# A LayerNorm mean taken off where a product leaves PSUM, instead of by extra matmuls and by centring the weights

## The chip, the cores and the metric

The kernel runs on one core of one Trainium2 chip. The metric is the time of one execution in device microseconds (us), the median of several. Engines are called by their names in the profile: PE is TensorE, PEld its weight loads, DVE VectorE, ACT ScalarE, POOL GpSimd, SP the engine whose queue issues nearly all DMAs.

## The reference, cut to what matters

A Nystrom attention with 32 landmarks per head feeds a LayerNorm and a two-layer MLP with a residual. There are 8 batches, 8 heads, 576 rows, head width 64, so d = 512 and 2048 hidden units.

```
A  = softmax(q @ k_lm.T);  Bm = softmax(q_lm @ k_lm.T);  C = softmax(q_lm @ k.T)
Z  = six steps of Z = 2 Z - Z @ Bm @ Z, from a scaled Bm.T
x  = heads of (A @ Z @ C @ v), side by side           # 576 x 512 per batch
mu = mean(x);  xn = (x - mu) / sqrt(var + 1e-6) * g_ln
out = x + max(xn @ w_ch1, 0) @ w_ch2
```

The kernel doesn't form xn. W1 below is w_ch1 with g_ln and a factor of 16 multiplied in, in fp16. With zt = the 32-row matrix Z (C v) of each head (called landmarks' rows below), x = A zt, so xn @ W1 is A times (zt @ W1), less the mean. The mean of a row of x is A times the row sums of zt, divided by 512. So the mean can be removed in any of three ways: W1's columns are centred (each column less its own mean over d); or the row sum of zt times the negative column mean of W1 is added to the product zt @ W1, as a rank-1 term; that term can be added by a matmul into the same accumulation, or by the operation that copies the product out of PSUM. The division by the deviation follows at the very end, in the copy of the second layer (`finish_block`), since the maximum with zero commutes with a positive factor.

## The kernel before, in words

**Attention, batch by batch or in pairs.** `attention0` treats batch 0 by itself at the start; `attention2` treats the sets (1), (2), (3, 4), (5, 6), (7). Each goes through: landmark scores `psb` and their softmax (`softmax_of`), scores against all keys `psec` (`scores_k`, exponential on ACT, transposed by DVE into `ecT`), the starting matrix (`gram_of`), the product of C and v (`product`, in PSUM tile `pscv`, closed by `product_done` into `cv`), six iterations (`iterate`: some matmuls of 32 x 32 into a PSUM bank, then one DVE operation that gives the next `st`), meanwhile the query scores `ea` (`scores_q`) and their division by their sums (`normalize`: a matmul `psd`, two activations `lns`, and one multiplication, by DVE for batch 1, by POOL for later sets), then `zt` and, from a second PSUM tile `pszc`, its masked form `zcbd`. `rows_of` multiplies `ea` by `zcbd` to get blocks of 128 rows of x; ACT copies each to `xblk`, and DVE takes its statistics (`block_done`: bn_stats and bn_aggr).

**The jobs of the next set.** `Coming` holds the loads (DMA on SP into six staging buffers `stg`), casts (POOL, to `nat`, with sums `asum` and `s` for some tensors) and jobs of a set: `turn` (a DVE transpose, and a small one of `s` with a reduction), `add_up` (two DVE reductions of 0.7 us), `spread` (a matmul on PE that reads the finished `part` tiles, copied by ACT to `lm`). `prepare(after, casts, jobs)` issues so many of each.

**The MLP.** `First(b)` is the first layer: `product_of_heads(f)` for four column groups f of 512 computes zt @ W1 into two PSUM banks (u = 0, 1: two groups of four heads), copied to `m16` in fp16; `chunk(m)`, m = 0 to 15, multiplies it by `ea` into a `psh` tile (pool `ps2`, two buffers, shared with psec, psea, psd, pscv, pszt and pszc), which ACT passes through the maximum with zero into `hT`. Chunk 4 f is the first that needs product f. `second_layer(b)` multiplies `hT` by `w2_16` for one block of 128 rows at a time, 16 matmuls of 512 columns into one PSUM bank, closed by `finish_block` (a DVE scalar_tensor_tensor on `xblk`, then the store on SP). `mlp()` interleaves second layer b with first layer b + 1 and is a stream of units; `fill(n)` draws n units of 512 columns from it. It draws from batch b + 1's first layer only when that batch's rows have begun (`ready`). What is left of the stream runs at the end.

**What sets the order.** All these instructions are kept in the order of the code, on each engine's queue. The list `steps` gives for every `yield` of a set's attention how much of the stream, how many casts and how many jobs follow. A `while` loop ahead of each set issues what jobs are left, with `fill(5)` after each. For batch 0 the order is written out: the loop over m = 0 to 15 issues chunk m, products 1, 2, 3 after chunks 1, 5, 8, W1's column means (`less_mean`: four matmuls with the constant -1/512, copied by ACT to `less(f)`), batch 1's jobs, batch 0's rows, and from m = 10 the second layer of blocks 0 and 1 (`blocks_0_and_1`, PSUM banks 0 and 1, held). Four PSUM banks are handed out in turn by `banks.take`; from batch 1's attention on, bank 3 belongs to the attention, and three are left.

**The mean.** For batches 0 and 1, `row_sums` computes the row sums of zt by four narrow matmuls with the constant `halves`, ACT copies them to `zsum`, and `product_of_heads` adds one matmul of 512 columns per u and f (`bank<-less,zsum` in the profile). During the first eight yields of batch 2's attention `center_w1` adds `less` to W1 in place, an eighth at a time, on DVE (`w<-w,less`); from batch 2 on the product needs no correction. ACT copies the product for u = 0 and for f = 0, DVE the others. The `less` tiles are two of the 14 buffers of `xpool`, in which the `xblk` tiles live; these buffers come free after the centring.

## Time and profile before

| | |
|---|---|
| median of 3 runs | 318.25 us (318.04 to 319.77) |
| the execution profiled | 318.92 us |
| its span, first to last instruction | 317.1 us |
| busy: PE, DVE, ACT, POOL | 280.5, 169.5, 181.7, 126.7 us |
| granted TensorE clock | 0.998 |
| HBM read, written | 36.70, 9.44 MB |

All durations below are from the one execution profiled; what lies outside its span is 1.82 us. In the profile's slices each digit is the busy share in tenths of a fortieth of the span (7.9 us). A row of a group gives engine and operation, the tiles written and read with their shapes, the count, the busy time and the mean duration, then the idle time just before such instructions and what ended it. Most rows name line 69 or 75, since helpers record every operation; the tiles tell them apart. A matmul row's mean (374 ns for 512 columns) is a latency; matmuls overlap, and the time from one to the next is shorter. In the lists in order of time, brackets hold the idle time of the engine before the instruction, and the instruction that ended it.

### The profile page before, as it was taken

What the parts mean: (1) busy time and instruction counts of PE and PEld (TensorE: products, weight loads), DVE (VectorE), ACT (ScalarE), POOL (GpSimd) and SP (SyncE); (2) the same over time, 40 slices, a digit from 0 to 9 for tenths busy, and PEclk for the clock granted to TensorE, in tenths of its full rate; (3) what the DMA queues carried; (4) which work ended last, traced back from release to release, by engine and by line L of the source; (5) the groups of instructions that cost most, each with busy time, mean ns of one, the idle gap of its engine ahead of it and who ended that gap; (6) DMA issues with size and microseconds to landing.
All of it is one profiled execution on the core that took longest, in us unless ns stands there. A gap on an engine that the chain in (4) does not pass through costs nothing. (4 is left out here: it accounts for less than half of the span.)

```text
span 317.1 us, 8209 instructions
## 1 busy us (share of the span) xinstructions
PE 280.5 (88%) x3439; PEld 149.7 (47%) x3439; DVE 169.5 (53%) x378; ACT 181.7 (57%) x315; POOL 126.7 (40%) x155
## 2 busy tenths in 40 slices
PE   8868996887885797887999999989999999999995
PEld 7534652344432344444544544545554456355544
DVE  2654946667898664336994972555442344121112
ACT  3479865178640674876668549576649465444300
POOL 5387748742469974653927423210003000100000
PEclk9999999999999999999999999999999999999999
DMA  7999997459527949600895261111111112213133
GB/s 258 388 389 386 388 235 285 128 131 293 192 55 233 294 118 321 198 2 9 207 277 166 55 169 33 33 35 35 33 37 34 35 34 50 51 33 68 33 87 82
DMA packets 23486, 46.68 MB, mean 147 GB/s; under 512 B 2324, under 2 KB 2584, under 8 KB 23448
## 3 DMA queue, kind: packets, MB, share of 16 engines
q1 hardware_dynamic: 23288, 46.02, 48.4%
q8 instruction: 27, 0.44, 0.6%
q10 hardware_dynamic: 160, 0.13, 0.2%
q14 instruction: 11, 0.09, 0.1%
HBM read 36.70 MB, written 9.44 MB: 146 GB/s over the span
## 5 line engine op out<-in xcount | busy, mean ns | idle before, releaser
L75 PE MATMUL bank<-w,hT 128*128 128x512 f16 (+1 forms) x592 | 151.0, 374 | 0.7 <-DVE m L69 0.4
L69 ACT ACTIVATE hT<-psh 128x576 f16<-128x576 f32 x128 | 81.5, 650 | 46.4 <-PE psh L75 45.4
L75 PE MATMUL psh<-ea,m 128*128 128x288 f16 x512 | 82.8, 286 | 6.4 <-ACT m L69 2.6
L75 PEld LDWEIGHTS <-hT 128*128 128x128 f16 x592 | 54.7, 98 | 48.5 <-issue 9.5
L75 PEld LDWEIGHTS <-m 128*128 128x128 f16 x512 | 49.0, 97 | 39.0 <-ACT m L69 6.3
L69 DVE SCALAR_TENSOR_TENSOR xblk<-bank,rstd,xblk 128x512 f32<-128x512 f32 (+1 forms) x37 | 26.8, 726 | 32.8 <-PE bank L75 32.7
L69 POOL CAST nat<-stg 128x1152 f16<-128x1152 f32 x28 | 33.1, 1194 | 23.8 <-DMA stg<-in_k_dram 9.9
L69 ACT COPY xblk<-bank 128x512 f32<-128x512 f32 (+1 forms) x40 | 23.3, 584 | 24.7 <-PE bank L75 24.6
L69 DVE BATCH_NORM_STATS2 six<-xblk 128x6 f32<-128x512 f32 x36 | 24.7, 686 | 23.0 <-ACT xblk L69 22.9
L69 POOL TENSOR_TENSOR ea<-ea,lns 128x576 f16<-128x576 f16 x12 | 15.4, 1283 | 51.5 <-ACT lns L69 45.1
L69 ACT CAST m<-bank 128x512 f16<-128x512 f32 x40 | 22.6, 586 | 16.5 <-PE bank L75 15.8
L69 DVE CAST m<-bank 128x512 f16<-128x512 f32 x24 | 16.4, 683 | 23.4 <-PE bank L75 21.3
L69 POOL CAST natv<-stg 128x1152 f16<-128x1152 f32 x16 | 18.3, 1162 | 26.5 <-DMA stg<-in_v_dram 23.9
L69 DVE SCALAR_TENSOR_TENSOR st<-st,bank 128x128 f16<-128x128 f16 (+2 forms) x36 | 11.3, 313 | 28.6 <-PE bank L75 28.6
L69 DVE TENSOR_REDUCE part<-xT 128x32 f16<-128x576 f16 x32 | 22.4, 742 | 0.1
L69 DVE STREAM_TRANSPOSE xT<-nat 128x576 uint32<-128x576 uint32 x28 | 21.3, 760 | 0.4 <-POOL nat L69 0.4
L75 PE MATMUL bank<-w,zt 64*32 64x512 f16 x256 | 17.0, 386 | 3.5 <-ACT xblk L69 2.3
L75 PE MATMUL bank<-zcbd,ea 128*128 128x256 f16 (+1 forms) x80 | 15.6, 274 | 3.4 <-ACT m L69 1.7
L69 POOL COPY hT<-hT 128x1024 f16<-128x1024 f16 x4 | 4.1, 1037 | 34.6 <-PE bank L75 26.2
L69 POOL TENSOR_TENSOR asum<-asum 128x256 f32<-128x256 f32 (+1 forms) x24 | 15.4, 643 | 1.9
L75 PEld LDWEIGHTS <-st 32*32 32x32 f16 x448 | 5.7, 89 | 19.2 <-DVE st L69 9.0
L75 PE MATMUL bank<-st 32*32 32x64 f16 (+1 forms) x384 | 9.3, 189 | 6.0 <-DVE st L69 5.9
(113 smaller groups left out, 264.4 us busy)
## 6 DMA issues: line engine op xcount, KB each, us to landing
stg<-in_q_dram SPq DMA_DIRECT2D x16, 576.0 KB, 6.4
stg<-in_k_dram SPq DMA_DIRECT2D x16, 576.0 KB, 7.0
out_dram<-xblk SPq DMA_DIRECT2D x70, 128.0 KB, 2.4
wstg<-in_moe_w_ch_dram SPq DMA_DIRECT2D x16, 512.0 KB, 7.1
stg<-in_v_dram SPq DMA_DIRECT2D x9, 576.0 KB, 5.7
stg<-in_v_dram SPq DMA_DIRECT2D x14, 288.0 KB, 5.5
out_dram<-xblk ACTq DMA_DIRECT2D x2, 64.0 KB, 2.2
out_dram<-xblk SPq DMA_DIRECT2D x2, 64.0 KB, 1.9
```

The costliest lines, as they stand in the source:

```text
L69: return lambda *args, **kw: keep(getattr(self.engine, op)(*args, **kw))
L75: keep(nc.tensor.matmul(o, l, r, start=start, stop=stop, tile_position=(rb, cb), skip_group_check=(skip or cb != 0)))
```

## The change

W1 is no longer centred and there are no row sums by matmul: `row_sums`, `center_w1` and the constant `halves` go. Instead each attention reduces its `pszc` tile over the 64 columns of a head on DVE (`zsum`, one fp32 number per row of the product), ahead of the `zcbd` operations, and `product_of_heads` leaves PSUM for all batches, f and u by one DVE scalar_tensor_tensor: `less(f)` times the row's `zsum`, plus the product. For batch 0's f = 0 this is cut into two halves of 256 columns. Since `less` is now read to the end, its tiles move to the pool of constants, and `xpool` has 12 buffers.

Around it: batch 1's normalisation goes from DVE to POOL. A `turn` job is held back while fewer than i + 3 casts (i being the number of its tensor; at most all of q and k) have been issued, and its step then issues no job. `product` is cut in two parts, j = 0 to 4 and 5 to 8, with a yield between. Batch 1's attention starts at m = 14 of batch 0's loop (scores), and its gram follows after the loop, ahead of the last eight matmuls of `blocks_0_and_1`; before, the scores came after block step 12 and the gram was the first yield of the loop over `steps`. The plan in `steps` has other counts. The diff, its contexts shortened:

```diff
-    halves = const.tile([P, 2], FP16, name="halves")
-    nc.gpsimd.tensor_copy(out=halves[:], in_=mask2[:])
-
     NV = 2
...
     w2_src = moe_w_ch2.rearrange("(m p) d -> p m d", p=P)
-    xpool = ctx.enter_context(tc.tile_pool(name="xpool", bufs=14))
-
-    less_ = [xpool.tile([P, 2, 512], FP16, name="less", tag="xblk") for _ in range(2)]
+    xpool = ctx.enter_context(tc.tile_pool(name="xpool", bufs=12))
+
+    less_ = [const.tile([P, 2, 512], FP16, name=f"less{i}") for i in range(2)]
...
                 MM(pszc[w][ds(cb, 32), :], st[sl, w, LM:], cv[sl, w, :], rb=32 * h, cb=cb)
-        heads[0] = (ea, zt, 0)
+        zsum = asm.tile([P, W], FP32, name="zsum", tag="zsum")
+        for w in range(W):
+            dve.tensor_reduce(out=zsum[:, w:w + 1], in_=pszc[w], axis=AX.X, op=ALU.add)
+        heads[0] = (ea, zt, [(w, zsum[:, w:w + 1]) for w in range(W)])
         yield "zt"
...
             if self.jobs:
-                f, i = self.jobs.pop(0)
+                f, i = self.jobs[0]
+                n = len(self.units)
+                if f == self.turn and 3 * n - len(self.casts) < min(i + 3, 2 * n):
+                    return
+                self.jobs.pop(0)
                 f(i)
...
-        def product(y):
+        def product(y, js=range(NJ)):
             if not pscv_:
...
             pscv = pscv_[0]
-            for j in range(NJ):
+            for j in js:
                 for r in range(2):
...
             for y in range(W // 2):
-                product(y)
+                product(y, range(0, 5))
+                yield False
+                product(y, range(5, NJ))
                 if y + 1 < W // 2:
...
             if W // 2 <= it < W // 2 + W:
-                normalize(ea[it - W // 2], dve if late else pool)
-            if late and it == 4:
-                product(0)
+                normalize(ea[it - W // 2], pool)
+            if late and it in (3, 4):
+                product(0, range(0, 5) if it == 3 else range(5, NJ))
             if late and it == 5:
...
         dve.tensor_copy(out=zt[:].rearrange("p r w l -> p r (w l)"), in_=pszt[:, :, 0:W * LM])
-        for i, b in enumerate(bs):
-            heads[b] = (ea[U * i:U * i + U], zt, U * i)
         pszc = ps2.tile([P, 2, 512], FP32, name="pszc", tag="p2")
...
                    rb=32 * p_, cb=cb)
+        zsum = asm.tile([P, 2, W // 2], FP32, name="zsum", tag="zsum")
+        dve.tensor_reduce(
+            out=zsum[:], in_=pszc[:, :, 0:D * (W // 2)].rearrange("p x (y e) -> p x y e", e=D),
+            axis=AX.X, op=ALU.add)
+        for i, b in enumerate(bs):
+            heads[b] = (ea[U * i:U * i + U], zt,
+                        [(w, zsum[:, w % 2, w // 2:w // 2 + 1]) for w in range(U * i, U * i + U)])
         for w in range(W):
...
-    def center_w1(f, c=0, n=KCH):
-        o = w1_16[:, ds(c, n), ts(f, 512)]
-        dve.tensor_tensor(out=o, in0=o, in1=less(f)[:, None, :].broadcast_to([P, n, 512]),
-                          op=ALU.add)
-
     class First:
...
             self.b, self.hT = b, hTs[b]
-            self.ea, self.zt, self.w0 = heads.pop(b)
-            self.m16, self.sums = {}, None
-
-        def row_sums(self):
-            pss = banks.take([P, U, 4, LM])
-            for u in range(U):
-                for e in range(2):
-                    MM(pss[:, u, ds(2 * (e ^ u), 2), :], halves[:, e:e + 1].broadcast_to([P, P]), self.zt[:, :, self.w0 + u, :])
-            self.sums = asm.tile([P, U, P], FP16, name="zsum", tag="zsum", bufs=1)
-            act(self.sums[:], pss.rearrange("p u k l -> p u (k l)"), AF.Copy, scale=1.0 / P)
+            self.ea, self.zt, self.units = heads.pop(b)
+            self.m16 = {}
...
                 for e in range(2):
-                    for u in range(U):
+                    for u, (w, _) in enumerate(self.units):
                         rows, cb = ds(64 * e, 64), 32 * (2 * (e ^ u) + r)
-                        MM(psm[u][ds(cb, 32), :], self.zt[rows, r, self.w0 + u, :],
-                           w1_16[rows, 2 * u + r, ts(f, 512)], rb=64 * e, cb=cb,
-                           stop=self.sums is None, skip=True)
-            for u in range(U):
-                if self.sums is not None:
-                    MM(psm[u], self.sums[:, u, :], less(f), start=False, skip=True)
-                if u == 0 or f == 0:
-                    scalar.copy(self.m16[f][:, u, :], psm[u])
-                else:
-                    dve.tensor_copy(out=self.m16[f][:, u, :], in_=psm[u])
+                        MM(psm[u][ds(cb, 32), :], self.zt[rows, r, w, :],
+                           w1_16[rows, 2 * u + r, ts(f, 512)], rb=64 * e, cb=cb, skip=True)
+            n = 2 if (self.b, f) == (0, 0) else 1
+            for part in range(n):
+                cols = ts(part, 512 // n)
+                for u, (_, total) in enumerate(self.units):
+                    dve.scalar_tensor_tensor(
+                        out=self.m16[f][:, u, cols], in0=less(f)[:, cols], scalar=total,
+                        in1=psm[u][:, cols], op0=ALU.mult, op1=ALU.add)
...
         l1 = First(b)
-        if b == 1:
-            l1.row_sums()
-            yield 256, 512
         l1.product_of_heads(0)
...
     l1 = First(0)
-    l1.row_sums()
     l1.product_of_heads(0)
...
             next(a0)
-        if 2 <= m < 10 or m == 13:
+        if 2 <= m < 10:
             b1.next_job()
+        if m == 13:
+            b1.next_job()
+        if m == 14:
+            assert not b1.jobs
+            banks.order.remove(3)
+            next(a1)
         if m >= 10:
...
     keep_tail(0)
+    next(a1)
     for m in range(12, MCH):
         blocks_0_and_1(m)
-        if m == 12:
-            assert not b1.jobs
-            banks.order.remove(3)
-            next(a1)
-            deviations(0)
+    deviations(0)
     for u in range(2):
...
-    steps = [[(4, 0, 0)] + 6 * [(3, 0, 0)] + [(4, 1, 0)] + 5 * [(6, 1, 1)]]
-    steps += [[(6, 1, 1)] * 2 + [(6, 1, 1)] * 6 + [(6, 1, 1)] + 5 * [(6, 1, 1)]]
-    steps += [4 * [(5, 1, 0)] + 6 * [(6, 1, 0)] + [(6, 0, 0)] + 10 * [(8, 1, 1)]]
-    steps += [4 * [(9, 1, 1)] + 6 * [(9, 1, 1)] + [(8, 1, 1)] + 10 * [(9, 1, 1)]]
-    steps += [2 * [(12, 0, 0)] + 6 * [(10, 0, 0)] + [(10, 0, 0)] + 5 * [(10, 0, 0)]]
+    steps = [6 * [(3, 0, 0)] + [(4, 0, 0), (4, 1, 0)] + 5 * [(6, 1, 1)]]
+    steps += [[(5, 1, 1)] * 3 + [(6, 1, 1)] * 6 + [(6, 1, 1)] + 5 * [(6, 1, 1)]]
+    steps += [2 * [(4, 1, 0)] + 4 * [(3, 0, 0)] + 6 * [(6, 1, 0)] + [(6, 1, 0)] + 10 * [(8, 1, 1)]]
+    steps += [2 * [(9, 1, 1)] + 4 * [(5, 0, 1)] + 6 * [(9, 1, 1)] + [(8, 1, 1)] + 10 * [(9, 1, 1)]]
+    steps += [3 * [(8, 0, 0)] + 6 * [(10, 0, 0)] + [(10, 0, 0)] + 5 * [(10, 0, 0)]]
     for c, after, plan in zip(sets, sets[1:] + [None], steps):
...
         attention = a1 if c is b1 else attention2(c.bs, c)
-        for i, ((count, casts, jobs), quiet[0]) in enumerate(zip(plan, attention)):
-            if c is sets[1] and i < 8:
-                center_w1(i // 2, 2 * (i % 2), 2)
+        for (count, casts, jobs), quiet[0] in zip(plan, attention):
             fill(count)
...
                 prepare(after, casts, jobs)
```

## The prediction

> **What bounds the kernel now.** I read the page's engine shares and slices first, then its chain.
>
> ```profile
> PE 280.5 (88%) x3439; PEld 149.7 (47%) x3439; DVE 169.5 (53%) x378; ACT 181.7 (57%) x315; POOL 126.7 (40%) x155
> ...
> PE   8868996887885797887999999989999999999995
> DVE  2654946667898664336994972555442344121112
> PE 39%; ACT 4%; issue 1%; DVE 1%; ACTq 0%
> ```
>
> TensorE is nearly full from 170 us on, and the chain runs on it; what it loses (317.1 - 280.5 = 36.6 us) lies mostly before. So a microsecond counts if it leaves TensorE's work or one of its waits. DVE has three stretches at 9 where it may set the pace. Next, the groups with shapes kept apart, for prices (the two columns after the count are busy us and mean ns).
>
> ```profile
> L69 DVE SCALAR_TENSOR_TENSOR xblk<-bank,rstd,xblk 128x512 f32<-128x512 f32 x35 | 25.8, 739 | 30.5 <-PE bank L75 30.4
> L69 ACT CAST m<-bank 128x512 f16<-128x512 f32 x40 | 22.6, 586 | 16.5 <-PE bank L75 15.8 <-ACT lm L69 0.6
> L69 DVE CAST m<-bank 128x512 f16<-128x512 f32 x24 | 16.4, 683 | 23.4 <-PE bank L75 21.3 <-ACT hT L69 2.0
> L69 DVE TENSOR_TENSOR w<-w,less 128x1024 f16<-128x1024 f16 x8 | 6.7, 840 | 0.0
> L75 PE MATMUL bank<-less,zsum 128*128 128x512 f16 x16 | 4.8, 384 | 0.0
> ```
>
> Last, TensorE's and DVE's instructions in order of time (start, duration, and in brackets the idle time before it and its releaser).
>
> ```profile
> 50.10 0.23 PE L75 MATMUL bank<-st 32*32 32x64 f16 x6 [1.30 <-DVE st L69]
> 55.17 0.24 PE L75 MATMUL bank<-st 32*32 32x64 f16 x8 [1.39 <-DVE st L69]
> 56.80 0.24 PE L75 MATMUL bank<-st 32*32 32x64 f16 x8 [0.64 <-DVE st L69]
> 76.90 0.38 PE L75 MATMUL bank<-part,spread 128*128 128x256 f16 x2 [1.21 <-DVE part L69]
> 93.33 0.24 PE L75 MATMUL bank<-st 32*32 32x64 f16 x8 [0.68 <-DVE st L69]
> 96.54 0.22 PE L75 MATMUL bank<-st 32*32 32x32 f16 x8 [1.57 <-DVE st L69]
> 99.45 0.24 PE L75 MATMUL pszt<-st,cv 32*64 32x32 f16 x8 [1.29 <-DVE st L69]
> 53.40 1.52 DVE L69 TENSOR_TENSOR ea<-ea,lns 128x576 f16<-128x576 f16 x1 [1.44 <-ACT lns L69]
> 55.04 1.51 DVE L69 TENSOR_TENSOR ea<-ea,lns 128x576 f16<-128x576 f16 x1
> ```
>
> The iterations of batches 1 and 2 wait for `st` behind other work in DVE's queue: the two normalisations (1.5 us each) in batch 1, the centring of W1 and the next set's jobs in batch 2. At 76.90 DVE is already late for batch 2's `spread`.
>
> **What the Trainium skill says.** VectorE: DVE Perf Modes, "The TRN2 errata", prices a DVE operation out of PSUM at 120 cycles plus one per element: 632 cycles, 0.66 us for 512. The trace is close, 0.683 for the copy and 0.739 for a scalar_tensor_tensor. PSUM — Partial Sum Buffer, "Engine vs sequencer instructions", says VectorE's queue is strict FIFO and matmuls go in program order; the waits above agree. TensorE: Matmul & The Clock Gate, "Back-to-back issue gap", gives N/2.4 + 2.5 ns, 216 ns for 512 columns; the last stretch agrees (64 of 512 and 32 of 256 in 17.32 us: 0.216 per 512). Perfetto Trace Analysis, "Optimizing Scalar/DVE Operations", says work may be moved off a saturated DVE; here it is moved onto it, so the question is where DVE is saturated.
>
> **The change, part by part**, against the profiled execution: 318.92 us, 1.82 of them outside the span of 317.1.
>
> *Rank-1 matmuls and row sums go.* 16 x 0.216 = 3.46 us of TensorE, half in batch 0 and half in batch 1, and about 0.3 for eight narrow matmuls on `halves`: -3.8. ScalarE loses the two `zsum` activations (0.8).
>
> *Centring goes.* Eight operations, 6.7 us of DVE at 81 to 100 us. The TensorE waits there that end with DVE are 0.70 (cv), 0.68, 1.57, 1.29 and 0.77 (zcbd): 5.0. The gate on `turn` jobs also takes out DVE's waits for POOL's `s` (0.96). Bounds -2.5 to -5; some steps still hold a 1.4 us `add_up`, so I take -4.2.
>
> *Batch 1's normalisation goes to POOL.* 1.39 + 0.64 of waits leave: -2.0. POOL's pair (1.28 each in its row) precedes batch 2's casts, which ran at 51 to 62 us and shift by about 5. Their cover: the first `turn` that reads them starts at 62.72 and is gated later still; uncovered they would cost up to 2. Behind them on SP stand loads that need the staging buffers; POOL's waits of 2.2 and 1.1 us for v at 62 to 67 take that up.
>
> *The gram goes up.* Its first half (psb, psec) is issued at m = 14 and its second before the last eight `blocks_0_and_1` matmuls (1.73 us), which cover csum, cinv and st. The 1.30 wait goes, but psec takes both ps2 buffers between chunks 14 and 15 (wait of about 0.65 for hT), and the two finishing operations (1.37) now stand in front of the first iteration's st. Bounds +0.5 to -1.5; taken -0.8. No DMA moves with it; the two stores of blocks 0 and 1 follow as before.
>
> *Copies become scalar_tensor_tensor.* ScalarE loses 40 x 0.586 = 22.6 us. DVE loses 16.4, 6.7 (centring) and 3.0 (normalising) and gains 62 x 0.74 + 4 halves x 0.48 (the row of 256 f32) = 47.8, and about 2.1 for seven `zsum` reductions (0.22 to 0.42 by the 64- to 256-wide rows): 169.5 becomes about 193. The form itself is not in the trace; bounds 0.68 (the copy) and 0.74, and back to back (two in 1.37) a pitch of 0.67. Where this meets a full DVE:
>
> - Batch 0 (24 to 41 us). DVE works through from 27.5 to 41.5 us already. Now 4 halves (1.7) fill its gap before 27.5, and six whole operations (4.0) replace three copies (1.9). Queued in the order of the code, product 3's first one comes after `add_up` 2 and ends near 36.1. Counting the bank takes, product 3 now sits in bank 0, which `blocks_0_and_1` needs; its first matmul was at 35.93. Batch 0's saving (1.73 + 0.15 of row sums) ends in that wait: +1.9.
> - Batch 1 (61 to 77 us). 8 x 0.67 for 3 x 0.62 is +3.5, the reduction +0.25; 1.35 fits into an idle of 2.48 us at 63.5 to 65.9, from which a `turn` (0.75) leaves. DVE is about 3.1 later at `spread`. TensorE issues 43 units of 512 columns before it where it was 35 (+1.7), and is freed of 2.0, so it arrives as before: the wait of 1.21 becomes 4.3. As 1.7 of work comes forward, the net is 1.4, and 3.4 with the 2.0 counted above. Bounds 1 to 5, since DVE can start sooner on what TensorE no longer delays: taken +2.8.
> - Batches 3 and 4's rows (142 to 172 us). DVE is idle 3.5 of 30 us and gets five operations of ScalarE's (3.4) and 0.4 of reduction; 1.35 fits into the wait of 1.96 before 146.01. `spread` at 170.50 has no slack (DVE's last part ends at 170.45). Bounds 0 to 3: taken +1.6.
> - Batch 2's rows: three operations (2.0) and a later job against 2.9 idle: +0.3 (0 to 1.5).
> - Starts of batches 4 to 7: the second matmul of chunk 0 came 1.18 after product 0 (103.70 to 104.88, on ScalarE), now about 1.5: 4 x 0.3 = +1.2.
>
> *The rest.* The split product holds a ps2 buffer through two more fills: +0.3 (0 to 1). A lighter ScalarE shortens waits on hT and xblk: -0.7 (0 to -1.5). xpool at 12 instead of 14: block 31 is taken at 225.9 with blocks 20 to 31 live, so it needs block 19's store, finished by DVE at 225.3 plus 2.4 to land. More units now run ahead of this point, so nothing is taken; if not, up to 2.
>
> Sum: -3.8 - 4.2 - 2.0 - 0.8 + 1.9 + 2.8 + 1.6 + 0.3 + 1.2 + 0.3 - 0.7 = -3.4, say 315.5 for the execution profiled. It stands 0.67 above the median of 318.25, so about 315.0.
>
> **Rivals.**
> - *DVE has the room.* In all it has 124 us free. If batches 1, 3 and 4 cost only 1 together, and batch 0 keeps its 1.9, it is 318.25 - 3.4 - 3.4 - 1.9 = 309.6 at the best, 312 if half. Against: queues are in order, and those stretches are full.
> - *Slower: `spread` waits behind the scalar_tensor_tensors.* At batch 1's and the (5, 6) set's `spread` TensorE stops until DVE's last `turn` is through. With the upper bounds there (5 and 3), and the waits in batch 2's iterations only half gone (-2.5) because `add_up` fills them, the sum is -3.4 + 2.2 + 1.4 + 1.7 = +1.9: 320. It decides once these waits grow by over 3.4 together. For: 76.90 and 170.50 are just where DVE is late or at par.
> - *Nothing gained.* The freed TensorE time turns into waits of the same length: 318.
>
> **How the numbers follow.** The forecast's case (313 to 316.6) has 0.38, the room 0.14, nothing gained 0.16, slower 0.32, with block 31's wait in it. A change under 0.5% (1.6 us) is about what a measurement of this kernel can't tell. Faster 0.52, same 0.16, slower 0.32. The range from 310.0 to 322.0 holds the room's half, and the slower case with another 2 us for block 31. The likeliest case's own range is 313 to 316.6.
>
> **What would show it.** Right: no `less,zsum` or `halves` rows and no `w<-w,less`; m only by DVE, 0.68 to 0.74 each, DVE near 193 us, ScalarE near 158; batch 1's iterations without DVE waits over 0.3; TensorE's wait at batch 2's `spread` grown to 3 or 4 us; a wait for bank 0 near 35 us. Wrong: a scalar_tensor_tensor over 0.8 us; DVE waits under 1 us at each `spread` (then faster than I say); waits for `st` in batch 2's iterations as before, or an xblk wait near 226 (then slower).

## The result, and the profile after

The changed kernel takes 332.51 us (median of 4 runs, 330.86 to 333.58), the kernel before 319.01 on the same chip (318.04 to 319.81): a ratio of 1.042, 95% interval 1.036 to 1.048. It is 4.2% slower; 315.0 was forecast, with 322 as the upper end. Here and below, medians are of all runs, while ratios leave out the runs more than 1.5% above the fastest of their kernel. The execution profiled took 333.58 us, its span 331.9.

The page of the changed kernel: shares, slices with the granted clock, and the chain.

```profile
PE 290.9 (88%) x3415; PEld 151.8 (46%) x3415; DVE 190.8 (58%) x417; ACT 160.8 (48%) x273; POOL 125.1 (38%) x156
...
PE   8988899795896977797988999889988999999995
...
DVE  2656974588489673247898644956743356343112
...
PEclk9956999989899799997999999999999999999999
...
PE 59%; DVE 21%; ACT 11%; DMA 4%; issue 4%; SPq 0%; ACTq 0%; DVEq 0%
```

The busy times of DVE and ACT are close to the forecast ones (193 and 158). The surprise stands in two places. TensorE's *busy* time rose by 10.4 us although 16 matmuls of 512 columns left, while its idle time rose by only 4.4 (36.6 to 41.0). And the row PEclk, all nines before, has holes: the granted clock was 0.958 over the span (0.998 before, where only the last 1.4 us ran at half).

The groups by shape, and the waits of TensorE (total us, times, longest), first of the changed kernel, then of the kernel before:

```profile
L69 DVE SCALAR_TENSOR_TENSOR m<-less,zsum,bank 128x512 f16<-128x512 f16 x62 | 43.2, 738 | 20.8 <-PE bank L75 20.6 <-ACT hT L69 0.2
```

```profile
PE psh L75 <- DVE m L69: 8.3, 16, 1.5
PE bank L75 <- DVE m L69: 5.1, 6, 1.4
PE bank L75 <- DVE part L69: 4.7, 2, 2.8
...
PE bank L75 <- DVE st L69: 1.6, 4, 0.6
```

```profile
PE bank L75 <- DVE st L69: 5.9, 6, 1.6
PE psh L75 <- ACT m L69: 2.6, 10, 0.5
PE bank L75 <- ACT m L69: 2.3, 5, 0.7
...
PE bank L75 <- DVE part L69: 1.2, 1, 1.2
```

The new operation costs the 0.74 us assumed. The rows for `less,zsum`, `halves` and `w<-w,less` are gone. Waits for `st` fell from 5.9 us (and 1.7 at pszt) to 1.6; waits for m are 13.4 us, where before it was 4.9 for ACT's m and about 0.4 for DVE's; waits for `part` 4.7, were 1.2.

The same instants as in the lists in order of time shown for the kernel before, now of the changed kernel, TensorE's queue:

```profile
64.09 0.30 PE L75 MATMUL psh<-ea,m 128*128 128x288 f16 x1 [0.85 <-DVE m L69]
64.75 0.54 PE L75 MATMUL psh<-ea,m 128*128 128x288 f16 x3 [0.36 <-DVE m L69]
...
67.47 1.17 PE L75 MATMUL psh<-ea,m 128*128 128x288 f16 x4
...
69.39 0.65 PE L75 MATMUL psh<-ea,m 128*128 128x288 f16 x4
...
82.03 0.39 PE L75 MATMUL bank<-part,spread 128*128 128x256 f16 x2 [2.85 <-DVE part L69]
...
100.37 0.22 PE L75 MATMUL bank<-st 32*32 32x32 f16 x8 [0.39 <-DVE st L69]
```

Batch 1's iterations wait for `st` only once (0.27 us, at 53.85), batch 2's 0.39 in all, and `spread` waits 2.85. At chunk 0 of batch 1 TensorE stands 0.85 and then 0.36 us for the two scalar_tensor_tensors in a row. Then, with no wait, four matmuls of a chunk take 1.17 us at 67.47 where they take 0.65 at 69.39.

Stretches of 3.4 us of the changed kernel (busy us of PE, PEld, DVE, ACT, POOL with counts, then the granted clock, DMA share, GB/s), in pairs: with a gap, and what followed.

```profile
61.80:65.20 3.40, 1.83 (x15) 0.74 (x15) 2.17 (x4) 0.58 (x1) 3.16 (x5) 1.00 0.64 159
65.20:68.60 3.40, 3.40 (x18) 1.29 (x17) 2.08 (x4) 1.13 (x2) 3.08 (x5) 0.50 1.04 287
78.80:82.20 3.40, 0.55 (x6) 0.33 (x4) 3.11 (x8) 0.87 (x2) 2.84 (x3) 1.00 1.02 392
82.20:85.60 3.40, 3.13 (x54) 1.67 (x56) 0.39 (x2) 2.00 (x4) 3.08 (x6) 0.51 0.95 362
...
150.50:153.90 3.40, 1.43 (x14) 0.64 (x15) 2.18 (x5) 0.65 (x1) 0.00 (x0) 1.00 0.67 174
153.90:157.30 3.40, 3.40 (x12) 1.74 (x12) 3.33 (x6) 1.24 (x2) 1.99 (x2) 0.51 0.00 0
```

In a stretch where TensorE was busy 1.83, 0.55 or 1.43 of 3.4 us nothing is wrong with the clock; the *next* stretch runs at half. There are five such falls before the end, 13.7 us long from 17.4 on and 3.4 us long near 65, 82, 110 and 154: 27.3 us, so 13.7 us of full-speed clock lost.

### The profile page after: what moved, and what is told of

Same layout as the page of the kernel before. It is cut to its first block, busy times and chain, and to the rows that moved or that the text cites. A ratio compares the mean times of both kernels' runs of the same rounds, so it can differ in the third digit from the quotient of the medians.

```text
span 331.9 us, 8161 instructions
## 1 busy us (share of the span) xinstructions
PE 290.9 (88%) x3415; PEld 151.8 (46%) x3415; DVE 190.8 (58%) x417; ACT 160.8 (48%) x273; POOL 125.1 (38%) x156
## 4 chain that ended last, share of the span: by engine, by line
PE 59%; DVE 21%; ACT 11%; DMA 4%; issue 4%; SPq 0%; ACTq 0%; DVEq 0%
PE bank L75 39%; PE psh L75 15%; DVE m L69 6%; ACT hT L69 5%; DVE part L69 4%; DVE six L69 3%; DMA wstg<-in_moe_w_ch_dram 3%; DVE xT L69 3%; ACT xblk L69 2%; DVE xblk L69 2%; PE psd L75 2%; DMA stg<-in_k_dram 1%; PE psec L75 1%; PE pscv L75 1%; ACT lns L69 1%
## 5 line engine op out<-in xcount | busy, mean ns | idle before, releaser
L75 PE MATMUL bank<-w,hT 128*128 128x512 f16 (+1 forms) x592 | 153.9, 378 | 1.6 <-DVE m L69 1.6
L75 PE MATMUL psh<-ea,m 128*128 128x288 f16 x512 | 87.5, 297 | 14.5 <-DVE m L69 8.3
L69 DVE SCALAR_TENSOR_TENSOR m<-less,zsum,bank 128x512 f16<-128x512 f16 (+1 forms) x66 | 44.8, 722 | 22.6 <-PE bank L75 20.6
L69 POOL CAST nat<-stg 128x1152 f16<-128x1152 f32 x28 | 31.9, 1144 | 34.6 <-DMA stg<-in_k_dram 13.7
L69 POOL TENSOR_TENSOR ea<-ea,lns 128x576 f16<-128x576 f16 x14 | 17.9, 1284 | 71.5 <-ACT lns L69 64.7
L75 PE MATMUL bank<-w,zt 64*32 64x512 f16 x256 | 19.3, 406 | 2.9 <-ACT xblk L69 1.8
L69 POOL TENSOR_TENSOR asum<-asum 128x256 f32<-128x256 f32 (+1 forms) x24 | 14.2, 590 | 1.9
L69 POOL TENSOR_TENSOR asum<-nat 128x512 f32<-128x512 f16 x12 | 13.8, 1152 | 1.0
L69 ACT ACTIVATE lns<-psd 128x576 f32<-128x576 f32 x16 | 10.4, 649 | 7.7 <-PE psd L75 7.6
L75 PEld LDWEIGHTS <-zt 64*32 64x32 f16 x256 | 5.1, 89 | 18.8 <-issue 17.4
```

The costliest lines, as they stand in the source:

```text
L69: return lambda *args, **kw: keep(getattr(self.engine, op)(*args, **kw))
L75: keep(nc.tensor.matmul(o, l, r, start=start, stop=stop, tile_position=(rb, cb), skip_group_check=(skip or cb != 0)))
```

## The experiments

Theories. *Queue*: TensorE waits for VectorE, whose queue got longer. Its two forms are *latency* (chunk 0 needs two operations in a row) and *load* (all that stands in VectorE's queue comes later). *Clock*: the waits are short, but each may cost the following 3.4 us half of their clock. *Order*: the moved work is to blame.

How times are compared. In every run the clock lost is (1 - granted clock) x span. Over the 133 runs of the kernel before that were made beside the experiments it is 2.9 us on average, and the time rises by 0.54 us for each microsecond lost (correlation 0.89). Four kernels below with 20 or 22 runs each give 0.56 to 0.61. So a stretch of 3.4 us at half clock (1.7 lost) costs about 1 us. "At full clock" below is the median of a kernel's runs with a granted clock of 1.000 where it has any; else, as an estimate, the mean of its times less 0.57 of the clock each lost ("by the line"). The kernel before: 318.4 at full clock (29 runs). It was run again beside each of the five rounds of experiments, with 318.1 to 318.8 at full clock, so a difference between kernels of different rounds is uncertain by some 0.5 us. The changed one lost 11.8 us on average: 325.6 by the line.

| | median us | ratio, 95% | lost, us | at full clock |
|---|---|---|---|---|
| changed | 332.5 | 1.042 (1.036-1.048) | 11.8 | 325.6 line |
| start filled | 332.4 | 1.043 (1.037-1.050) | 11.3 | 326.3 line |
| waits filled | 329.4 | 1.034 (1.029-1.038) | 0.6 | 329.3 |
| mean alone | 326.9 | 1.024 (1.018-1.031) | 8.1 | 322.1 line |
| order alone | 322.1 | 1.010 (1.007-1.012) | 3.6 | 320.0 |
| fewer fills | 327.4 | 1.021 (1.012-1.030) | 3.9 | 325.1 line |
| f = 0 by ACT | 327.9 | 1.025 (1.019-1.031) | 6.9 | 323.7 line |
| half load | 325.2 | 1.017 (1.010-1.023) | 9.5 | 319.7 line |
| batch 1's order | 325.7 | 1.019 (1.013-1.026) | 5.6 | 322.6 line |
| fitted fills | 325.1 | 1.013 (1.008-1.017) | 1.7 | 324.0 |
| fitted fills, half load | 317.9 | 0.994 (0.991-0.997) | 1.1 | 317.7 |
| before, no mean | 314.5 | 0.978 (0.974-0.982) | 5.3 | 311.7 line |
| order, no mean | 318.4 | 0.993 (0.990-0.996) | 5.5 | 315.5 line |
| POOL normalise | 318.7 | 0.996 (0.993-0.999) | 3.8 | 316.8 |
| order, DVE normalise | 322.8 | 1.011 (1.006-1.016) | 3.7 | 321.1 line |
| mean in 2 batches | 322.6 | 1.007 (1.005-1.010) | 10.1 | 317.0 line |
| POOL normalise, filled | 317.4 | 0.993 (0.991-0.996) | 1.3 | 317.0 |
| mean in 2, filled | 317.0 | 0.992 (0.990-0.995) | 1.6 | 316.1 |

Five of these kernels leave the mean in, in all features or in part of them: f = 0 by ACT, the two with half load and the two with no mean. Their output is not the reference's; they stand here only for their times.

### Is it the clock? Start filled, waits filled

The fill is a few matmuls of a constant, written to a PSUM region that the next real matmul overwrites:

```diff
+    def warm_next(n, cols=256):
+        i = next(i for i in banks.order if i not in banks.held)
+        idle = banks.view(i, [P, 512])
+        for _ in range(n):
+            MM(idle[:, 0:cols], zeros[:, 0:P], zeros[:, 0:cols])
...
                 product(it - 2)
+                if it == 2:
+                    warm_next(8)
                 lns.append(divisors(ea[it - 2]))
```

> The changed kernel, with 8 matmuls of 256 columns of a constant tile (their product is overwritten and used by nothing) set ahead of batch 0's divisors, where TensorE stood 1.25 us before its clock fell to half for 13.5 us. Clock theory (short waits let the granted clock fall, and the half-clock stretches are the loss): the stretch from 17.7 to 31.2 us is gone and with it half of its length, 5 to 7 us: 326 to 328 us, mean clock near 0.98; the four later stretches stay. Queue theory (the loss is the time that TensorE waits for VectorE's m and part): nothing changes, 331 to 334.

Measured: 332.41 us. In the execution profiled the first fall is gone as expected, but its cost is not gone from the time. The slices of this run:

```profile
PEclk9999999898698799997999999999999999999999
```

The four later falls stay, and two of them now last twice as long: 3.4, 6.8, 6.8 and 3.4 us from 64, 81, 105 and 153 us on. The mean loss over the runs is 11.3 us where it was 11.8. So one fall taken away need not shorten the sum of them. Only the profiled executions show where the falls lie; whether the first fall was there in all runs of the changed kernel is not known. The clock theory in the form "each fall costs its half" failed here.

```diff
             psl = banks.take([P, 2, 8, LM])
             for half in range(2):
+                if half == 0:
+                    for _ in range(10):
+                        MM(psl[:, 0, :, :].rearrange("p k c -> p (k c)"), zeros[:, 0:P], zeros[:])
...
             psh = ps2.tile([P, 2, 512], FP32, name="psh", tag="p2")
+            if m == 0:
+                for _ in range(8):
+                    MM(psh[:, 0, 0:256], zeros[:, 0:P], zeros[:])
```

> As the kernel before this one, and with 10 such unused matmuls ahead of each spread and 8 ahead of chunk 0 of every batch, that is inside the waits for part and for m, which are left as long as they are. Clock theory: no stretch under 0.9 is left, mean clock 0.99 or more, 317 to 321 us. Queue theory: the waits are as long as ever and the unused matmuls come on top where a wait was shorter than they are: 332 to 336.

Measured: 329.43, clock 0.995 to 1.000. Both numbers missed: the clock was held, and the time fell by only 3 us. The fill is in the way where the wait was short or absent: the five spreads that had no wait got 1.26 us of unused matmuls each, and each chunk 0 1.04 us, whether it waited or not. So this run shows that the clock can be held, not what it is worth.

### Mean alone, order alone

```diff
-            for u in range(U):
-                if self.sums is not None:
-                    MM(psm[u], self.sums[:, u, :], less(f), start=False, skip=True)
...
+                for u, (_, total) in enumerate(self.units):
+                    dve.scalar_tensor_tensor(
+                        out=self.m16[f][:, u, cols], in0=less(f)[:, cols], scalar=total,
+                        in1=psm[u][:, cols], op0=ALU.mult, op1=ALU.add)
...
-            if c is sets[1] and i < 8:
-                center_w1(i // 2, 2 * (i % 2), 2)
```

The plan of steps, the gram, the normalise and the product stay as in the kernel before.

> The mean's part of the change alone (scalar_tensor_tensor on VectorE, reductions of zsum, less in tiles of its own, 12 block buffers, no rank-1 matmuls, no centring of W1), in the order of work of the kernel before: its plan of steps, batch 1's gram where it was, its normalise on VectorE, no bound on the early jobs, one product of the scores in one piece. Queue theory: VectorE's queue delays part and st as well as m, with batch 1's normalise still in it: slower than the changed kernel's 332.5, 333 to 338. Clock theory: slow only if a wait lets the clock fall; with the waits for m ahead of each chunk 0 still there, 325 to 335 with a mean clock of 0.95 to 0.98. If the order of work is to blame (it was the reordering that made the waits): 316 to 320, clock at 0.99.

> The rest of the change alone: batch 1's gram earlier, its normalise on GpSimd, the product of the scores in two pieces, the early jobs held back, the new plan of steps, on the mean as the kernel before takes it (row sums, rank-1 matmuls, centring of W1, ScalarE and VectorE copies, 14 block buffers). Queue theory and clock theory both: the waits for m return to the kernel before's, clock 0.99 or more, and batch 1's normalise off VectorE gains 1 to 4 us: 314 to 318 us. If the order of work is to blame: over 325.

The second is the converse: the diff above not made, the rest of the change made. Measured: 326.93 and 322.08; at full clock +3.7 and +1.6 against 318.4. Both parts slow the kernel, and the clock loss comes with the mean (8.1 us against 3.6), which fits the clock theory (325 to 335). The order alone fits no theory: it was to gain 1 to 4 us, or to lose over 6. TensorE's waits in its run say why it did not:

```profile
PE bank L75 <- DVE part L69: 4.2, 2, 2.5
PE bank L75 <- DVE st L69: 3.9, 5, 1.6
PE psh L75 <- ACT m L69: 3.9, 11, 1.3
```

`st` fell by 2.0 us from 5.9, `part` rose by 3.0 from 1.2, ACT's m by 1.3. Batch 1's rows begin at 57.5 us where they began at 60.8; batch 2's `spread`, after a wait of 2.48 for 1.21, at 74.9 for 76.9; and batch 2's scores at 78.3 for 78.5. So of the 3.3 us that batch 1 gained, 1.3 are waited for at the `spread`. Nearly all the rest went between there and the scores, where this execution ran at half clock from 74.7 to 78.1.

### Latency or load; fewer fills; batch 1's order

```diff
+            if self.bs[0] == 2 or (self.bs[0] == 3 and y == 1):
+                for _ in range(8):
+                    MM(psl[:, 0, :, :].rearrange("p k c -> p (k c)"), zeros[:, 0:P], zeros[:])
...
+            if m == 0 and self.b in (1, 2, 3):
+                for _ in range(5):
+                    MM(psh[:, 0, 0:256], zeros[:, 0:P], zeros[:])
```

> The changed kernel with unused matmuls only where TensorE waited longer than they take: 8 ahead of batch 0's divisors, 8 ahead of the spread of batch 2 and of the second spread of (3, 4), 5 ahead of chunk 0 of batches 1, 2 and 3. Clock theory: the stretches at half clock near 65, 83, 110 and 154 us go, mean clock 0.985 or more, and the time comes to what the runs so far give for full clock (a line through the changed kernel's times against the clock time it lost, from the first fill run, ends at 326.0): 325.5 to 328. Queue theory alone: 331 to 334, whatever the clock does.

Measured: 327.4, but in two groups: 325.8 and 324.5 with the clock at 0.995 and 0.999, 328.9 and 330.1 at 0.979. The same program differs by over 4 us between the two.

```diff
                 for u, (_, total) in enumerate(self.units):
+                    to = self.m16[f]
+                    if f == 0:
+                        scalar.copy(to[:, u, cols], psm[u][:, cols])
+                        to = self.m16[1]
                     dve.scalar_tensor_tensor(
-                        out=self.m16[f][:, u, cols], in0=less(f)[:, cols], scalar=total,
+                        out=to[:, u, cols], in0=less(f)[:, cols], scalar=total,
```

> The changed kernel with VectorE's load kept and its latency ahead of chunk 0 taken away: of each batch's first 512 hidden features m is written by two ScalarE copies (the mean is left in for these), while VectorE makes the same scalar_tensor_tensors into a tile that is written over. Latency theory (the loss is TensorE standing at chunk 0 until two scalar_tensor_tensors in a row are done, 0.85 + 0.36 us a batch against 0.37 before): 8 x 0.84 = 6.7 us less waiting, and the clock drops that follow chunk 0 (65, 110 and 154 us) go: 322 to 326. Load theory (what counts is VectorE's total work, which delays part and the later m): 330 to 333.

```diff
+                    if f and u == 0:
+                        scalar.copy(self.m16[f][:, u, cols], psm[u][:, cols])
+                        continue
                     dve.scalar_tensor_tensor(
```

> The other way round: chunk 0's two scalar_tensor_tensors stay on VectorE, and of the other three products of each batch the first half goes to a plain ScalarE copy (the mean is left in there): 24 scalar_tensor_tensors of 0.72 us less on VectorE, 17 us. Load theory: the waits for part (4.7 us) and for m ahead of the attention's matmuls (5.1 us) shrink to those of the kernel before, and the clock drop at 83 us goes: 323 to 327. Latency theory: the waits at chunk 0 stay, 330 to 333.

Measured: 327.9 without the latency at chunk 0 and 325.2 with half the load at the other products; by the line 323.7 and 319.7, against 325.6. Load is worth about 6 us, latency about 2 at full clock (and 3 us of clock loss, 11.8 to 6.9 us times 0.57). Both kernels also give ScalarE copies that the changed kernel doesn't have. Neither theory holds alone; load is the larger.

```diff
-                product(y, range(0, 5))
-                yield False
-                product(y, range(5, NJ))
+                product(y)
...
-    steps += [[(5, 1, 1)] * 3 + [(6, 1, 1)] * 6 + [(6, 1, 1)] + 5 * [(6, 1, 1)]]
+    steps += [[(6, 1, 1)] * 2 + [(6, 1, 1)] * 6 + [(6, 1, 1)] + 5 * [(6, 1, 1)]]
...
```

This is against the order alone; the plans of the sets after batch 2 go back likewise.

> The kernel before with only what the change does to the order up to batch 1: gram earlier, normalise on GpSimd, early jobs held back, batch 1's own plan; the plans of batch 2 on and the product of the scores in one piece as before. If the 2.3 us that the whole reordering costs at full clock come from the later plans: 317 to 318.5, at best faster than both kernels. If they come from batch 1's part: 320 to 322. Where batch 2's part is what limits, the 3 us that batch 1 gains come back as a longer wait at its spread (2.5 us in the run of the order alone, 1.2 before).

Measured: 325.7, 322.6 by the line, so the old plans made it worse, not better. That the later plans cost the 1.6 us is refuted. As expected `spread` waited 2.48 us. Batch 2's rows began 3.7 us earlier than in the kernel before (98.3 for 102.0 us), and the lead was gone by the scores of (3, 4) (114.6 for 114.7); later the (5, 6) set took 5.5 us more from scores to rows, with a stretch of 3.4 us at half clock in it.

### What the clock, the load and the mean are worth

```diff
-                for _ in range(8):
+                for _ in range(16 if self.bs[0] == 2 else 12):
...
-                for _ in range(5):
+                for _ in range(9 if self.b == 2 else 6):
```

This is against the fewer fills.

> The changed kernel with unused matmuls sized closer to the waits: 16 ahead of batch 2's spread, 12 ahead of the second spread of (3, 4), 6 ahead of chunk 0 of batches 1 and 3, 9 for batch 2, 8 ahead of batch 0's divisors. Clock theory: clock at 0.99 or more in nearly every run, and the time at 324.5 to 326.5, which is where the lines through the changed kernel and the two fill runs end; so about 6 of the 13.5 us lost were the clock. If the fill itself costs: over 327 with the clock at 1.0.

Measured: 325.08, clock 0.989 to 1.000; 324.0 in the two runs at 1.000. With fills fitted to the waits the changed kernel is 7.4 us faster than without (runs of different rounds), and the forecast of the line holds. TensorE at chunk 0 of batch 1 in this run:

```profile
62.14 0.82 PE L75 MATMUL psh<-zeros 128*128 128x256 f16 x6
63.16 0.30 PE L75 MATMUL psh<-ea,m 128*128 128x288 f16 x1 [0.20 <-DVE m L69]
63.82 0.54 PE L75 MATMUL psh<-ea,m 128*128 128x288 f16 x3 [0.36 <-DVE m L69]
```

The wait of 0.85 is full of unused matmuls, m comes when it came (1.24 us after the last real matmul began, as at 64.09 in the changed kernel), and no fall follows there. Nothing of use was added, so the gain is the clock's: 7.4 us as measured, 5.8 by the line for the 10.1 us of clock regained.

The next one adds the diff of the half load:

> The kernel before this one, and of the second to fourth product of each batch the first half goes to a plain ScalarE copy (the mean is left in there), 17 us less on VectorE. Load theory: the half-load run's own line ends at 319.6 to 320.9 for full clock: 319 to 321.5 here. If that line misled and load is worth little: 323 to 326.

Measured: 317.9, clock 0.989 to 1.000. Against the run before it: 324.0 to 317.7 at full clock, 6.3 us for 24 of the scalar_tensor_tensors. Its slices:

```profile
DVE  2567954686688753169995375655443354321112
PEclk9999999999999999999999999999999999999999
```

```diff
     l1 = First(0)
-    l1.row_sums()
...
-            if c is sets[1] and i < 8:
-                center_w1(i // 2, 2 * (i % 2), 2)
```

> The kernel before without row sums, rank-1 matmuls and centring of W1; its copies, order and buffers as they are. The mean is left in everywhere, so this is the most that any treatment of the mean could gain on this order. The prediction took 3.8 us for the rank-1 part and 4.2 us for the centring: 310 to 311. If the time that they take is covered by batch 2's wait for its sums, as the run of the order alone hints (3 us gained by batch 1, none left at batch 2's spread): 316 to 318.

> The same on the changed order: the order alone (322.1; 320.1 at full clock) without row sums, rank-1 matmuls and centring, the mean left in everywhere. If the removal is worth what the prediction took: 312 to 314. If it is covered: 318 to 320. Against the changed kernel (325.6 at full clock) the difference is the price of 66 scalar_tensor_tensors on VectorE with the order held.

Measured: 314.5 and 318.4; by the line 311.7 and 315.5. On the old order the removal is worth 6.7 us (318.4 to 311.7), on the changed one 4.5 (320.0 to 315.5). The prediction's gain was real, within 1 to 4 us; on the changed order it lies between the two expectations. With the order held, the scalar_tensor_tensors then cost 324.0 - 315.5 = 8.5 us (10.1 by the line), and on the old order 322.1 - 311.7 = 10.4.

### The parts of the order, and a version that is faster

```diff
-                normalize(ea[it - W // 2], dve if late else pool)
+                normalize(ea[it - W // 2], pool)
```

> The kernel before with batch 1's normalise on GpSimd and nothing else. If the normalise is worth what the prediction took (2.0 us less waiting of batch 1's iterations for st): 316 to 317 at full clock, against 318.1 for the kernel before. If the time gained is only waited for at batch 2's spread: 317.5 to 318.5 at full clock. If GpSimd's queue is what costs (its casts of the next batches stand behind the normalise): 319.5 or more.

This is the kernel before with that one line. Measured: 318.7; 316.8 at full clock against 318.2 for the 7 full-clock runs of the kernel before beside it: 1.4 us faster, ratio 0.996 (0.993 to 0.999). Its TensorE in the last iterations of batch 1:

```profile
54.58 0.24 PE L75 MATMUL bank<-st 32*32 32x64 f16 x8
54.75 0.75 PE L75 MATMUL pscv<-natv,ecT 64*32 64x65 f16 x72
55.43 0.82 PE L75 MATMUL bank<-w,hT 128*128 128x512 f16 x3
56.19 0.22 PE L75 MATMUL bank<-st 32*32 32x32 f16 x8
```

The waits of 1.39 and 0.64 us are gone. At batch 2's `spread` the wait is 1.21 us, as long as before, and that set's scores begin at 76.3 for 78.5. So this gain is kept.

> The order alone, with batch 1's normalise left on VectorE. If the normalise on GpSimd is what costs: 317 to 318.5 at full clock, against 320.1 with it on GpSimd. If the earlier gram and the later plans cost: 320 to 322.5.

Its diff is that line turned back in the order alone. Measured: 322.8, 321.1 by the line. The order without the normalise loses 2.7 us against 318.4; the normalise gives back 1.1.

```diff
-                if self.sums is not None:
-                    MM(psm[u], self.sums[:, u, :], less(f), start=False, skip=True)
-                if u == 0 or f == 0:
+                if self.zs is not None:
...
+                        dve.scalar_tensor_tensor(
+                            out=self.m16[f][:, u, cols], in0=less(f)[:, cols], scalar=self.zs[u],
+                            in1=psm[u][:, cols], op0=ALU.mult, op1=ALU.add)
+                elif u == 0 or f == 0:
```

Here `zs`, the row sums, exists for batches 0 and 1 only.

> The kernel before with the row sums and rank-1 matmuls of batches 0 and 1 replaced by 16 scalar_tensor_tensors on VectorE and two reductions; W1 centred and everything else as before. Load theory with the price that the runs give (10 us for 66 scalar_tensor_tensors, so 0.15 us each, 2.4 us for 16) against the rank-1 part's worth (2 to 4 us): 316.5 to 318.5 at full clock. If the waits at chunk 0 of batches 0 and 1 and batch 2's part make more of it: 319.5 or more.

Measured: 322.6 on the median with 10.1 us of clock lost, 317.0 by the line. At full clock that would be 1.2 us less than the kernel before beside it (318.2); as it ran, it is 0.7% slower (the ratio, 1.007). Two stretches of this run and what followed:

```profile
63.20:66.60 3.40, 1.85 (x9) 0.69 (x9) 2.37 (x5) 1.05 (x2) 1.16 (x1) 1.00 0.97 237
66.60:70.00 3.40, 3.27 (x17) 1.53 (x17) 3.25 (x6) 0.98 (x3) 2.32 (x2) 0.50 0.29 100
76.80:80.20 3.40, 0.98 (x9) 0.81 (x9) 3.33 (x9) 0.98 (x3) 2.13 (x2) 1.00 1.03 388
80.20:87.10 6.90, 5.93 (x122) 3.25 (x119) 3.58 (x11) 4.76 (x9) 2.93 (x5) 0.51 0.64 243
```

Whether that 317.0 can be had was the last question.

```diff
+    idle_at = {(1, 0): 9, (2, 4): 5, (2, 5): 11}
...
+            if (bs[0], it) in idle_at:
+                warm_next(idle_at[bs[0], it])
             st = iterate(p1, st, it, W)
```

> The kernel before with batch 1's normalise on GpSimd (318.7 on the median, 316.6 at full clock) and unused matmuls in its longest waits: 8 ahead of batch 0's divisors, 9 ahead of batch 1's first iteration, 9 at batch 2's spread, 5 and 11 at its last two iterations, 9 at zt. Clock theory: clock at 0.995 or more, median 316.5 to 317.3. If the clock is no cause, or the fill costs as much as it saves: 318 to 319.5.

> The same fill, with 6 more unused matmuls ahead of chunk 0 of batches 0 and 1 and 16 at batch 2's spread, in the kernel with the mean by scalar_tensor_tensor in batches 0 and 1 and batch 1's normalise on GpSimd. Clock theory: the line of the run without fill ends at 316.9, less 1.2 for the normalise: 315 to 317 with the clock at 0.99. If the scalar_tensor_tensors in batches 0 and 1 cost by VectorE's queue what the rank-1 part cost on TensorE: 316.5 to 318. If the clock is no cause: 320 to 322.

Measured: 317.4 (clock 0.987 to 1.000) and 317.0 (0.984 to 1.000), ratios 0.993 (0.991 to 0.996) and 0.992 (0.990 to 0.995). Both are 0.7 to 0.8% faster than the kernel before, and cannot be told from each other. The same mean that was 0.7% slower than the kernel before without the fill is 0.8% faster with it and the normalise; the normalise is worth about 1.4 us of this.

## Why the prediction was wrong, by its own steps

**Two steps failed. One is not in the sum: every wait was priced at its own length, and TensorE's clock at nothing. The other is in its terms: the new order of work was taken as a gain and is a cost, and the scalar_tensor_tensors' waits were priced too low.** The clock alone doesn't explain the miss: even at full clock the changed kernel takes 324.0 to 325.6, above the upper end of 322.

The clock first. The page of the kernel before showed 0.998 and a row of nines, and its own waits of 1.2 to 1.6 us had not cost the clock in that execution. But its trace already has eleven stretches of 3.4 us in which TensorE was busy for only 1.84 to 2.44 us. So the sum treats a new wait of 0.85 us as 0.85 us. The run with fitted fills shows 5.8 to 7.4 us that hang on the clock alone (all of the 11.8 lost, times 0.57, is 6.7), of the 13.5 between the two kernels; the kernel before pays about 1.7 of its own (2.9 us lost, times 0.57). The Trainium skill has the mechanism, in TensorE: Matmul & The Clock Gate, "What's actually happening": the array's clock is halved after an idle window of about 3.4 us and comes back after a busy one, and these windows run freely, whenever the kernel starts. The trace agrees on the half, the 3.4 us (3.4, 6.8 and 13.7 us are one, two and four of them) and the shift between runs. The page's "HAM oscillation" puts the danger at idle gaps of over 3.4 us; here the longest was 2.85, and waits of 0.35, 0.85 and 0.36 us in one stretch (61.8 to 65.2) were enough. The measurement decides.

The rest, 324.0 to 325.6 at full clock against 318.4, is 5.6 to 7.2 us slower where the sum has -3.4, so its terms are off by 9 to 10.6 together. One by one:

- *Rank-1 and row sums -3.8, centring -4.2.* Together -8.0; measured -6.7 on the old order, -4.5 on the changed one. Right in kind; that the changed order had already taken a part of it from batches 1 and 2, which could not be taken twice, is likely and not shown.
- *Batch 1's normalisation -2.0.* Right in kind, a third too large or more: -1.4 on the old order, -1.1 on the new, and POOL's later casts delayed nothing: `spread` waited the same 1.21.
- *The gram goes up -0.8, the split product +0.3.* Wrong in sign: the order without the normalise costs 2.7. The prediction priced the gram's own waits and took the new plan of steps at nothing. Of batch 1's gain 1.3 us are waited for at batch 2's `spread` (1.21 to 2.48 us). Which of the moved counts costs the rest was not found; the old plans with the new batch 1 are worse still.
- *Batch 0 +1.9.* Right in place: product 3 sits in bank 0 and its wait is 1.40 us, at 39.7.
- *Batch 1's `spread` +2.8.* The wait grew from 1.21 to 2.85, not to 4.3. Right in place. But it leaves TensorE 0.55 us of work in a stretch of 3.4, and the next one is at half clock.
- *Batches 3 and 4 +1.6, batch 2 +0.3, starts of batches 4 to 7 +1.2.* Too small. The chunks' waits for m are 8.3 us, 5.7 more than for ACT's m before, and not only from batch 4 on; the second `spread` of (3, 4) waits 1.86 where it was 0.47. With 0.7 off for ScalarE, the prediction's costs of the scalar_tensor_tensors are 7.1 us; measured 8.5 to 10.4.
- *xpool at 12.* Right: near 240 us there is a wait of 0.54 for m and none for xblk.

So of the sum's terms the order's was wrong by some 4 us, the gain short by 1 to 4 and the scalar_tensor_tensors' cost by 1 to 3, and the clock added 4 to 6 net of what it takes from the kernel before. Of the rivals, "slower: `spread` waits behind the scalar_tensor_tensors" was right at one of its two places. Its own condition, growth of over 3.4 us together, did not come: batch 2's `spread` waits 1.6 us more and the (5, 6) set's (at 177.1 and 181.6) not at all, while the (3, 4) set's second one, which it did not name, waits 1.4 more. And its 320 left out the clock too. None of the signs named for a slower end came (0.738 us for the operation, 0.39 of `st` waits in batch 2, no xblk wait), and nothing in the list looked at the clock's row. What is argued and not shown: why just these stretches made the clock fall and others did not.

## What to carry to other kernels

A short wait on TensorE has two prices: its length, and the clock of the next microseconds. When a change moves work to another engine, look for stretches of a few microseconds that a new wait would leave half empty, and hold the clock there with unused matmuls that are shorter than the wait; longer ones cost what they take. And compare versions at equal clock too: one kernel here was, by the line, 1.2 us better than the one that it came from at full clock and 0.7% slower as it ran.

## What the runs showed of the hardware that was not expected

- In the changed kernel the clock fell in pieces of 3.4 us (one or four), always to 0.50, after stretches of 3.4 us in which TensorE was busy 0.55 to 2.25 us, with no single wait over 2.85 us.
- Within each of the 19 traces the falls begin whole steps of 3.41 us apart, and where this grid of steps lies differs from run to run; in the changed kernel they begin 0, 14, 19, 27 and 40 steps after 17.4 us. Of all steps of these grids that ran at full clock, from 8 us on, the clock fell after all 15 in which TensorE was busy for under 1.5 us, after none of the 1479 with 2.45 us or more, and after 21 of the 163 in between. So in between busy time alone does not decide: in the changed kernel 1.54 us in 116.4 to 119.8 was followed by full clock, and in the kernel before 1.87 us in 52.9 to 56.3 as well.
- A stretch at half clock costs about 1 us of the 1.7 lost: 0.54 to 0.61 us for each microsecond lost, in five kernels with 20 to 133 runs.
- Taking away one fall (start filled) left the loss as it was, 11.3 us for 11.8; in the execution profiled, two of the other four lasted twice as long.
